# The start of a dense-SiLU backward kernel: x in four tiles on two queues, fewer warm-up matmuls

## The chip, the cores and the metric

The kernel runs on one core of one Trainium2 chip. The metric is device time in microseconds (us), as the median of several executions. The profile of one execution gives a span (first to last instruction); the measured time is about 1.8 us longer, so the two are not mixed here.

## The reference

```python
B, S, D, F = 1, 2048, 640, 1536          # all bfloat16

def _fwd_reference(x, w1, w2):
    h = silu(einsum("bsd,df->bsf", x, w1))
    return einsum("bsf,fd->bsd", h, w2)

def reference(x, w1, w2, grad_out):
    out, vjp = jax.vjp(_fwd_reference, x, w1, w2)
    return (out, *vjp(grad_out))          # out, grad x, grad w1, grad w2
```

## The kernel before

The rows of x are worked off in four chunks of 512. For each chunk the kernel computes h = x·w1, its SiLU and derivative, the output, and the gradient of x; two long stages for the weight gradients follow. Only the start concerns us. The first chunk of x is loaded in its natural layout, transposed on TensorE, and then the first matmuls of h can run. Warm-up matmuls on a tile of zeros keep TensorE busy while the first data travel.

```python
NWARM = 36
warm = cpool.tile([P, P], dt_in, name="warm")
nc.vector.memset(warm[:], 0.0)
warm_a = cpool.tile([P, 1], FP32, name="warm_a")
nc.scalar.activation(warm_a[:], warm[:, 0:1], ACT.Silu)        # loads the Silu table
wp = ps_h.tile([P, SC], FP32, name="wp", tag="hp")
for i in range(NWARM):
    nc.tensor.matmul(wp[:, 0:P], lhsT=warm[:], rhs=warm[:], start=True, stop=True)
# ... cut ...
nc.sync.dma_start(out=x_nat[:, 0:STC, :], in_=x_v[:, 0:STC, :])              # 512 rows, 640 KB
nc.sync.dma_start(out=w1_nat[:, :, 0:FH], in_=w1_v[:, :, 0:FH])              # 320 KB
nc.sync.dma_start(out=w1_nat[:, :, FH:FC], in_=w1_v[:, :, FH:FC])
# ... cut: rest of w1, w2, transposed loads ...
for dt_ in range(DT):                                  # pe_xT: 5 x 4 transposes
    tp = ps_h.tile([P, 4, P], dt_in, name="tp", tag="hp")
    for j in range(4):
        nc.tensor.transpose(tp[:, j, :], x_nat[:, j, dt_ * P:(dt_ + 1) * P], ident[:])
    # DVE (even dt_) or ACT (odd dt_) copies tp to xT[:, dt_, 0:512]
# h_group(ft): five 128x512 matmuls over dt_, then two ACT and two DVE instructions
# ... cut ...
if c == 1:
    for j in range(0, ST, STC):                        # rows of grad_out, four loads
        nc.sync.dma_start(out=go_nat[:, j:j + STC, :], in_=go_v[:, j:j + STC, :])
```

## Time and profile before

| | before |
|---|---|
| median of the first 6 runs | 321.89 us (321.7 to 322.4) |
| span of the profiled run | 320.1 us |
| TensorE (PE) busy | 316.2 us, 99% |
| last row of x's first chunk landed | 5.25 us |
| first matmul of h | 6.42 us |
| end of the last matmul, to the end of the span | 317.43 us, 2.68 us |

These are lines of the page of the profiled run: span, busy times, and the chain of work that ended last, by engine. (PE is TensorE's matmuls, PEld its weight loads, DVE VectorE, ACT ScalarE, POOL GpSimd; SPq is SyncE's sequencer, which issues DMAs and waits; x20 counts instructions; L125 is a line of the kernel. "issue" is time in which the engine waited for nothing that the profile shows. Of the tiles, x_nat is x as loaded, tp what the transposes write, xT the transposed x, wp what the warm-up writes and hp the sums of the matmuls.)

```profile
span 320.1 us, 3590 instructions
PE 316.2 (99%) x1512; PEld 146.7 (46%) x1512; DVE 101.9 (32%) x179; ACT 78.3 (24%) x140; POOL 0.7 (0%) x6
...
PE 98%; DMA 1%; DVE 0%; issue 0%; DVEq 0%
```

TensorE works all the time, and the chain runs through it. The chain in order of time (start in us, length in us, what) shows the only other piece of size, at the very start:

```profile
0.74 4.51 DMA x_nat<-in_x_dram
5.30 1.29 PE tp L125 x20
6.59 12.95 PE hp L151 x60
```

The timeline of PE for the same stretch (start, length, engine, line, output and inputs; in brackets the idle time before and its releaser):

```profile
0.99 4.02 PE L97 MATMUL wp<-warm 128*128 128x128 bf16 x36 [0.99 <-DVE warm L92]
5.30 1.29 PE L125 MATMUL tp<-ident,x_nat 128*128 128x128 bf16 x20 [0.28 <-DMA x_nat<-in_x_dram]
6.42 1.25 PE L151 MATMUL hp<-xT,w_nat 128*128 128x512 bf16 x5
```

Read it so: 36 warm-up matmuls take 4.02 us and start 107 ns apart. The twenty transposes have the same shape and start 56 ns apart: TensorE's clock went from half to full rate in between. Below, "the clock is released" means this change. From 6.42 us the matmuls follow each other without a gap until 317.43 us, those of 128x512 every 216 ns. First h matmul to last matmul is 311.01 us. So the span is a sum of three terms: **start of h + 311.0 + end**.

### The profile page before, as it was taken

How to read it: one execution, taken by the hardware profiler on the slowest of the kernel's cores; microseconds unless marked ns; L12 is line 12 of the kernel's file. 1: busy time of each engine (PE TensorE's matmuls, PEld its weight loads, DVE VectorE, ACT ScalarE, POOL GpSimd, SP SyncE). 2: the span in 40 equal slices, each digit the busy share in tenths (PEclk: the TensorE clock that was granted, in tenths of full speed). 3: DMA queues.
4: the chain of work that ended last, by engine and by line, in shares of the span. 5: the costliest groups of instructions: out<-in, count | busy, mean ns of one | idle time of the engine just before them, and what ended most of it. 6: DMA issues, size and time to landing. Idle time of an engine off the chain costs nothing.

```text
span 320.1 us, 3590 instructions
## 1 busy us (share of the span) xinstructions
PE 316.2 (99%) x1512; PEld 146.7 (46%) x1512; DVE 101.9 (32%) x179; ACT 78.3 (24%) x140; POOL 0.7 (0%) x6
## 2 busy tenths in 40 slices
PE   8999999999999999999999999999999999999996
PEld 7444444444444444444444444444444444444443
DVE  1871551477510087710147751000000100001001
ACT  3960001555201255401154520110100001001100
POOL 0000000000000000000000000000000000000000
DMA  8999999999999855291635079809999999994111
GB/s 232 314 194 190 252 222 274 341 263 309 262 286 296 227 180 151 69 324 63 175 109 146 2 247 269 224 16 301 260 241 242 269 209 342 238 293 166 52 37 47
DMA packets 149200, 66.69 MB, mean 208 GB/s; under 512 B 112576, under 2 KB 149184, under 8 KB 149184
## 3 DMA queue, kind: packets, MB, share of 16 engines
q1 hardware_dynamic: 149184, 66.46, 81.8%
q8 instruction: 12, 0.20, 0.3%
q14 instruction: 4, 0.03, 0.0%
HBM read 9.18 MB, written 28.97 MB: 119 GB/s over the span
## 4 chain that ended last, share of the span: by engine, by line
PE 98%; DMA 1%; DVE 0%; issue 0%; DVEq 0%
PE hp L186 32%; PE hp L151 16%; PE hp L276 16%; PE hp L170 16%; PE hp L324 15%; DMA x_nat<-in_x_dram 1%; PE hp L306 1%; PE tp L125 0%; DVE g_2364 L317 0%; DVEq L317 0%
## 5 line engine op out<-in xcount | busy, mean ns | idle before, releaser
L151 PE MATMUL hp<-xT,w_nat 128*128 128x512 bf16 x240 | 56.9, 379 | 0.0
L170 PE MATMUL hp<-goT,w2T 128*128 128x512 bf16 x240 | 56.9, 379 | 0.0
L186 PE MATMUL hp<-aT,w_nat 128*128 128x512 bf16 x240 | 52.5, 379 | 0.0
L186 PE MATMUL hp<-ghT,w1T 128*128 128x512 bf16 x240 | 52.5, 379 | 0.0
L276 PE MATMUL hp<-a_blk,go_nat 128*128 128x512 bf16 x240 | 52.0, 379 | 0.0
L324 PE MATMUL hp<-gh_blk,x_nat 128*128 128x512 bf16 x224 | 48.5, 379 | 0.0
L194 ACT ACTIVATE oT<-hp 128x512 bf16<-128x512 f32 x24 | 14.3, 597 | 110.0 <-PE hp L186 110.0
L186 PEld LDWEIGHTS <-w_nat 128*128 128x128 bf16 x240 | 23.5, 98 | 28.3
L170 PEld LDWEIGHTS <-w2T 128*128 128x128 bf16 x240 | 23.5, 98 | 28.3
L276 PEld LDWEIGHTS <-go_nat 128*128 128x128 bf16 x240 | 23.5, 98 | 28.3
L186 PEld LDWEIGHTS <-w1T 128*128 128x128 bf16 x240 | 23.4, 98 | 28.4
L158 ACT ACTIVATE aT<-hp 128x512 bf16<-128x512 f32 x48 | 28.7, 598 | 31.1 <-PE hp L151 31.1
L151 PEld LDWEIGHTS <-w_nat 128*128 128x128 bf16 x240 | 23.4, 98 | 28.1
L196 DVE CAST oT<-hp 128x512 bf16<-128x512 f32 x16 | 11.1, 692 | 78.0 <-PE hp L186 78.0
L177 DVE SCALAR_TENSOR_TENSOR ghT<-ghT,hp 128x512 bf16<-128x512 bf16 x48 | 32.5, 683 | 7.3 <-PE hp L170 7.3
L324 PEld LDWEIGHTS <-x_nat 128*128 128x128 bf16 x224 | 21.9, 98 | 26.4
L163 DVE SCALAR_TENSOR_TENSOR ghT<-aT,v 128x512 bf16<-128x512 bf16 x48 | 33.0, 688 | 0.6
L162 DVE TENSOR_SCALAR v<-t 128x512 bf16<-128x512 f32 x48 | 20.5, 427 | 28.5 <-ACT t L160 28.5
L160 ACT ACTIVATE t<-hp 128x512 f32<-128x512 f32 x48 | 28.4, 591 | 0.0
L286 DVE CAST g2T<-hp 128x512 bf16<-128x512 f32 x7 | 4.8, 692 | 46.1 <-PE hp L276 46.1
L284 ACT ACTIVATE g2T<-hp 128x512 bf16<-128x512 f32 x8 | 4.8, 598 | 47.0 <-PE hp L276 47.0
L97 PE MATMUL wp<-warm 128*128 128x128 bf16 x36 | 4.0, 313 | 1.0 <-DVE warm L92 1.0
(32 smaller groups left out, 27.0 us busy)
## 6 DMA issues: line engine op xcount, KB each, us to landing
aT_scr<-aT SPq DMA_DIRECT2D x4, 1536.0 KB, 6.2
ghT_scr<-ghT SPq DMA_DIRECT2D x4, 1536.0 KB, 10.1
out_dram<-o_sb SPq DMA_DIRECT2D x8, 640.0 KB, 3.4
x_nat<-in_x_dram SPq DMA_DIRECT2D x4, 640.0 KB, 4.7
oT_scr<-oT SPq DMA_DIRECT2D x4, 640.0 KB, 4.3
go_nat<-in_grad_out_dram SPq DMA_DIRECT2D x4, 640.0 KB, 7.1
gxT_scr<-oT SPq DMA_DIRECT2D x4, 640.0 KB, 4.7
w_nat<-in_w_dram SPq DMA_DIRECT2D x2, 960.0 KB, 11.3
```

The costliest lines, as they stand in the source:

```text
L151: nc.tensor.matmul(hp[:], lhsT=w1_nat[:, dt_, ft * P:(ft + 1) * P], rhs=xT[:, dt_, :], start=(dt_ == 0), stop=(dt_ == DT - 1),)
L158: nc.scalar.activation(aT[:, ft, :], hp[:], ACT.Silu)
L160: nc.scalar.activation(t[:], hp[:], ACT.Tanh, scale=0.5)
L162: nc.vector.tensor_scalar(out=v[:], in0=t[:], scalar1=-0.5, scalar2=0.5, op0=ALU.mult, op1=ALU.add)
L163: nc.vector.scalar_tensor_tensor(out=ghT[:, ft, :], in0=aT[:, ft, :], scalar=1.0, in1=v[:], op0=ALU.subtract, op1=ALU.mult)
L170: nc.tensor.matmul(gp[:], lhsT=w2T[:, dt_, ft * P:(ft + 1) * P], rhs=goT[:, dt_, :], start=(dt_ == 0), stop=(dt_ == DT - 1),)
L177: nc.vector.scalar_tensor_tensor(out=ghT[:, ft, :], in0=ghT[:, ft, :], scalar=1.0, in1=gp[:], op0=ALU.add, op1=ALU.mult)
L186: nc.tensor.matmul(op_[:], lhsT=w_all[:, ft, dt_ * P:(dt_ + 1) * P], rhs=rhs_all[:, ft, :], start=(ft == 0), stop=(ft == FT - 1),)
L194: nc.scalar.activation(oT[:, dt_, :], op_[:], ACT.Copy)
L196: nc.vector.tensor_copy(out=oT[:, dt_, :], in_=op_[:])
L276: nc.tensor.matmul(gp[:], lhsT=go_nat[:, st, dt_ * P:(dt_ + 1) * P], rhs=a_blk[:, st, :], start=(st == 0), stop=(st == ST - 1),)
L324: nc.tensor.matmul(gp[:], lhsT=x_nat[:, st, dt_ * P:(dt_ + 1) * P], rhs=gh_blk[:, st, :], start=(st == 0), stop=(st == ST - 1),)
```

## The change

The intent is to start h earlier. x comes in four 128-row tiles on two queues (SyncE and ScalarE issue two each), and each tile is transposed as it lands. The first piece of w1 comes as rows 0 and 1 of five, then rows 2 to 4. The warm-up needs no memset, since it reads a constant that exists already, and has 26 matmuls. Four filler matmuls follow the transposes. Here is the diff, cut to its core.

```diff
-    NWARM = 36
+    NWARM = 26
+    NFILL = 4
-        warm = cpool.tile([P, P], dt_in, name="warm")
-        nc.vector.memset(warm[:], 0.0)
+        warm = nc.const_aps.tensor(1.0, (P, P), dt_in)
...
-        nc.sync.dma_start(out=x_nat[:, 0:STC, :], in_=x_v[:, 0:STC, :])
-        nc.sync.dma_start(out=w1_nat[:, :, 0:FH], in_=w1_v[:, :, 0:FH])
+        load_x_tile(nc.sync, 0)
+        load_x_tile(nc.scalar, 1)
+        load_x_tile(nc.sync, 2)
+        load_x_tile(nc.scalar, 3)
+        for lo, hi in ((0, 2), (2, DT)):
+            nc.sync.dma_start(out=w1_nat[:, lo:hi, 0:FH], in_=w1_v[:, lo:hi, 0:FH])
...
+        nc.scalar.activation(warm_a[:], warm[:, 0:1], ACT.Silu)     # moved behind the loads
...
-        xT_next = pe_xT(0, 1)
+        DS = 3
+        def pe_x_tile(xT, st):
+            for lo, hi, copy in ((0, DS, nc.vector.tensor_copy), (DS, DT, nc.scalar.copy)):
+                tp = ps_h.tile([P, hi - lo, P], dt_in, name="tp", tag="hp")
+                for dt_ in range(lo, hi):
+                    nc.tensor.transpose(tp[:, dt_ - lo, :], x_nat[:, st, dt_ * P:(dt_ + 1) * P], ident[:])
+                copy(out=xT[:, lo:hi, st * P:(st + 1) * P], in_=tp[:])
+        for st in range(STC):
+            pe_x_tile(xT_next, st)
+        for i in range(NFILL):
+            nc.tensor.matmul(wp[:, 0:P], lhsT=ident[:], rhs=x_nat[:, STC - 1, 0:P], start=True, stop=True)
```

## The prediction

> **What bounds the kernel now.** TensorE, everywhere but in the first 6.4 us. The page gives PE 316.2 us busy of a 320.1 us span (99%). The chain of waits that ended last is 98% PE; before it stand 4.51 us for the first load of x (0.74 to 5.25 us) and 1.29 us of twenty transposes (from 5.30 us). From there PE runs without a gap to 317.4 us, successive 128x512 matmuls starting 216 ns apart, granted clock 1.00. The waits of PE show only two: 1.0 us for the memset of the warm tile, 0.3 us for x. The change touches the start alone: it can only shift this stream by a fraction of a microsecond, 0.1 to 0.3% of the time.
>
> **What it changes, costed.** In the timeline the 36 warm-up matmuls start at 0.99 us, 107 ns apart, about half rate; the transposes after them 56 ns apart. The 640 KB of x land at 5.25 us; the first w1 piece (320 KB), behind it on the same queue, at about 6.35 us; the first real matmul starts at 6.42 us. So x with its transposes, and w1, limit the start almost together.
>
> 1. Without the memset (DVE, 0.82 to 0.93 us) the warm-up starts 0.2 us earlier; 26 of them (2.8 us) end near 3.6 us. That alone gains nothing.
> 2. x in four 160 KB tiles on two queues: the same bytes at about 350 GB/s, so the last tile should still land at 5.0 to 5.2 us, the first two near 3.8 us. Fifteen transposes happen before the last tile lands. After it remain three transposes before the DVE copy, PE latency and that copy (128x512 took 425 ns, so I estimate 0.35 us for 128x384): first real matmul 0.75 us after the last landing, near 5.8 us.
> 3. w1's rows 0 and 1 of five (128 KB) should land near 5.7 us, the rest near 6.2 us. Two matmuls (0.43 us) run before the rest is needed: an equivalent start near 5.8 us as well.
> 4. Four filler matmuls cost about 0.22 us of PE, hidden behind the DVE copy. Silu's table load (1.28 us) moves behind two DMA issues on ScalarE (a 128-descriptor issue took 0.33 us elsewhere): not critical.
>
> The whole gain is on the critical path, as nothing later waits for DMA: w1's third piece lands at 9.4 us and is needed at about 10.2. I expect the stream 0.5 us earlier.
>
> **Prediction: 321.4 us** (before 321.95), 80% range 320.9 to 322.2. Chances: faster by over 2%: 0.005; within 2%: 0.985; slower by over 2%: 0.01.
>
> **What would show it.** First tile landing before 4 us; transposes from about 3.8 to 5.4 us; first h matmul near 5.8 us, perhaps a gap up to 0.3 us after its second; no PE gaps later; the tail unchanged.
>
> **What would make it wrong.** First, the clock. The Trainium skill, "TensorE: Matmul & The Clock Gate", Part 1, has the array at half clock until about 3.4 us of sustained activity; the trace agrees (107 ns apart up to 4.7 us, 56 ns from 5.3 us). With ten warm-up matmuls fewer and gaps between tiles, full rate may come later; each h matmul at half rate costs about 0.21 us more, so 2 us of delay costs 1 us and turns gain into loss. I give this 15 to 20%. Second, "DMA: Bandwidth & Descriptors", "Issuing engines are not separate DMA queues", has both queues share the same engines: if w1's packets interleave with the last x tiles, these land after 5.25 us and the gain shrinks to 0.2 us.

## The result, and the profile after

| | before | after |
|---|---|---|
| median, 6 runs each | 321.89 us (321.7 to 322.4) | 321.91 us (321.5 to 322.27) |
| ratio after/before | | 0.9999, 95% interval 0.9987 to 1.0012 |
| last row of x's first chunk landed | 5.25 us | 5.50 us |
| first matmul of h | 6.42 us | 6.48 us |
| first h matmul to end of last matmul | 311.01 us | 311.00 us |
| end of last matmul to end of span | 2.68 us | 2.98 us |

A ratio is the mean time of one kernel's runs over that of the other's runs of the same rounds, so it is not quite the ratio of the medians quoted. No gain shows. The interval reaches from 0.42 us faster to 0.39 us slower (0.9987 and 1.0012 of 321.9 us): a small gain could hide in it, but hardly the predicted 0.5 us. The time lies inside the predicted range. The page of after, and its chain at the start:

```profile
span 320.5 us, 3556 instructions
PE 314.0 (98%) x1477; PEld 145.9 (46%) x1506; DVE 101.8 (32%) x179; ACT 78.6 (25%) x142; POOL 0.7 (0%) x6
...
PE 97%; DMA 1%; issue 1%; ACT 0%; SPq 0%; DVE 0%; DVEq 0%
```

```profile
1.19 4.09 DMA x_nat<-in_x_dram
5.27 0.05 issue
5.32 0.47 PE tp L148 x5
5.78 0.02 issue
5.81 0.66 ACT xT L149 x2
6.47 0.01 issue
6.48 0.38 PE hp L161
```

PE has 1477 matmuls here but 1506 weight loads. The records of 29 matmuls are missing, about every fiftieth, and each leaves a gap of twice 216 ns between its neighbours. That is no stall, because the 311.00 us are intact. The timeline of PE:

```profile
0.78 2.93 PE L96 MATMUL wp<-const-bfloat16-1.0 128*128 128x128 bf16 x26 [0.78 <-PEq L362]
3.62 0.74 PE L148 MATMUL tp<-ident,x_nat 128*128 128x128 bf16 x10
5.32 0.73 PE L148 MATMUL tp<-ident,x_nat 128*128 128x128 bf16 x10 [0.96 <-DMA x_nat<-in_x_dram]
5.88 0.39 PE L154 MATMUL wp<-x_nat,ident 128*128 128x128 bf16 x4
6.48 1.24 PE L161 MATMUL hp<-xT,w_nat 128*128 128x512 bf16 x4 [0.21 <-ACT xT L149]
```

The view names ScalarE (ACT) as what released h, and so does the chain. It puts a wait for several semaphores down to the one that came last; point 5 of the account shows that VectorE's copy set the start.

In this one profile the two first tiles are transposed early, as intended. But tile 2 landed at 5.27 us and tile 3 at 5.50 us. A load counts as landed when its sixteen DMA completions are in. For tile 3 fifteen of them were in by 4.95 us, and the last came 0.55 us later; before, this lag was 0.26 us. From the last landing to the first h matmul the new order needs 0.98 us (6.48 − 5.50) where the old one needed 1.17 (6.42 − 5.25). The later landing eats that gain, and the start of h is 0.06 us late.

The end of the span was 0.30 us longer, although the change does not touch it. These are the waits of SyncE's queue at the end, before and then after (who waited for what: us in total, times, longest):

```profile
SPq L363 <- PEq L363: 0.6, 2, 0.4
SPq L363 <- DMA out_dram<-g_2364: 0.5, 1, 0.5
SPq L318 <- DVE g_2364 L317: 0.3, 1, 0.3
SPq L363 <- DMA out_dram<-g_2344: 0.3, 1, 0.3
```

```profile
SPq L373 <- DMA out_dram<-g_2366: 1.1, 1, 1.1
SPq L373 <- PEq L373: 0.6, 2, 0.4
SPq L328 <- DVE g_2366 L327: 0.3, 1, 0.3
```

Before, SyncE waits for the second last store (0.3 us) and then for the last one (0.5 us). After, it waits 1.1 us for the last store at once. The longer wait itself is harmless, for it ends at the same moment (below). What counts is what SyncE still has to do after it.

### The profile page after: what moved, and what is told of

The parts are those of the page before. It is cut to its first block, busy times and chain, and to the rows that moved or that the text cites. A ratio compares the mean times of both kernels' runs of the same rounds, so it can differ in the third digit from the quotient of the medians.

```text
span 320.5 us, 3556 instructions
## 1 busy us (share of the span) xinstructions
PE 314.0 (98%) x1477; PEld 145.9 (46%) x1506; DVE 101.8 (32%) x179; ACT 78.6 (25%) x142; POOL 0.7 (0%) x6
## 4 chain that ended last, share of the span: by engine, by line
PE 97%; DMA 1%; issue 1%; ACT 0%; SPq 0%; DVE 0%; DVEq 0%
PE hp L196 32%; PE hp L180 16%; PE hp L286 16%; PE hp L161 16%; PE hp L334 15%; DMA x_nat<-in_x_dram 1%; PE hp L316 1%; ACT xT L149 0%; PE tp L148 0%; SPq L123 0%; DVE g_2366 L327 0%; DVEq L327 0%
## 5 line engine op out<-in xcount | busy, mean ns | idle before, releaser
L343 ACT ACTIVATE g_2140<-hp 128x512 bf16<-128x512 f32 x1 | 0.6, 597 | 13.6 <-DMA out_dram<-g_2077 13.6
```

## The experiments

Five theories were in play. **A**: a late DMA engine sets the landing of the last tile, however x is split. **B**: the second queue lets w1's packets pass x. **C**: something else than x holds the start. **D**: TensorE's clock is released at a moment that differs from run to run, and the new start is more exposed to it. **E**: the order of the last waits makes the end longer.

### after_again: the changed kernel once more

> The changed kernel once more, for a second profile. In the first one the last x tile landed at 5.50 us (15 of its 16 engine completions by 4.95 us) and the first h matmul started at 6.48 us, against 5.25 and 6.42 before. Both theories expect the same again: last x tile at 5.3 to 5.6 us, one completion 0.4 to 0.7 us behind the other fifteen, first h matmul at 6.4 to 6.6 us, time within 0.1% of before. If landings scatter by more than 0.3 us between the two profiles, single profiles can't settle this.

Measured: 322.09 us median (321.75 to 322.5, 5 runs), ratio 1.0004 (0.9992 to 1.0017). In its profile the last tile landed at 4.78 us, its last completion only 0.09 us behind the other fifteen, and h started at 5.99 us. The expectation missed on both counts: the landing moved by 0.72 us between two profiles of one kernel. So the late landing of the first profile is one draw of a lottery and not a property of the change, and single profiles can't settle the case. Even with h starting 0.43 us earlier than in the first profile of before (6.42 − 5.99), the span was 319.97 us against 320.11, only 0.14 us less: the end took 2.98 us again.

### x_one_queue: all four tiles on one queue

```diff
-        load_x_tile(nc.scalar, 1)
+        load_x_tile(nc.sync, 1)
-        load_x_tile(nc.scalar, 3)
+        load_x_tile(nc.sync, 3)
```

> All four x tiles on the SP queue, ahead of w1. Theory A (one slow DMA engine of sixteen sets the landing of the last tile, however x is split): last tile still at 5.2 to 5.5 us, first h matmul at 6.3 to 6.5 us or later if issuing four tiles in a row (0.4 us each) delays w1; time unchanged within 0.1%. Theory B (the second queue lets packets of w1 pass the last tile): with strict order the last tile lands near 5.0 us, its late completion is gone, first h matmul near 6.0 us, 0.4 us faster.

Measured: 322.82 us median, ratio 1.0026 (1.0012 to 1.004). The last tile landed at 5.51 us and h started at 6.44 us, about as A said, but A's unchanged time did not come. Strict order did not make x earlier in this profile. That alone would not settle B, for the fourth tile was also issued 0.9 us later (2.12 us for 1.20 in the second profile of after). The packets in the traces say more: x comes in packets of 1280 bytes, the first 512 columns of w1 in packets of 512. Before the last x packet started, 352 packets of 512 bytes had started here, 174 and 261 in the two profiles of before, 531 and 140 in the two of after. So w1 passes the tail of x on one queue as well as on two. And in the first profile of after, where x was late, the last twelve x packets of one chain (4.31 to 4.88 us) take 55 ns each and start 51 to 57 ns apart, from the two queues in turn. That is the pace of one engine that still has only x to do. So w1 did not hold that tile up at the end. What moved was w1. Its second piece was issued at 3.08 us for 2.17 us in the second profile of after, and landed at 7.41 us for 6.26. The start of h, at 6.44 us, then stalls:

```profile
6.44 0.38 PE L161 MATMUL hp<-xT,w_nat 128*128 128x512 bf16 x1 [0.21 <-ACT xT L149]
7.45 0.39 PE L161 MATMUL hp<-xT,w_nat 128*128 128x512 bf16 x1 [0.63 <-DMA w_nat<-in_w_dram]
```

The Trainium skill says in "DMA: Bandwidth & Descriptors", section "Issuing engines are not separate DMA queues", that a second issuing engine only saves the issue time, "which is usually small relative to the DMA itself". The trace agrees that issue time is saved (about 0.4 us a tile). At this start one queue instead of two cost 0.7 us on the mean (322.81 us against 322.11 of after_again, run against the same rounds of before). The wait for w1 in this profile is a cause that the trace shows; that it is all of the 0.7 us is not shown.

### x_two_tiles_only: tiles 2 and 3 taken off the path

The transposes of tiles 2 and 3 read tiles 0 and 1, so the result is wrong.

```diff
-  nc.tensor.transpose(tp[:, dt_ - lo, :], x_nat[:, st, dt_ * P:(dt_ + 1) * P], ident[:])
+  nc.tensor.transpose(tp[:, dt_ - lo, :], x_nat[:, st % 2, dt_ * P:(dt_ + 1) * P], ident[:])
-  ... rhs=x_nat[:, STC - 1, 0:P], ...
+  ... rhs=x_nat[:, 1, 0:P], ...
```

> Wrong result on purpose: transposes of tiles 2 and 3 read tiles 0 and 1 (landed at 3.6 and 3.7 us); the loads stay. If the landing of tiles 2 and 3 holds the start (both theories above), the first h matmul moves from 6.48 to about 5.8 us (first w1 piece landed at 5.78), with a wait of about 0.2 us before the third matmul (second w1 piece at 6.43): 0.4 us faster, about 0.12%. If the copies, the clock or w1 hold it (theory C), the h stream starts within 0.15 us of 6.48 us and the time stays.

Measured: 322.01 us median (321.53 to 322.23), ratio 0.9998 (0.9985 to 1.0011). In the profile, which is of the 321.53 us run, h starts at 5.63 us (about 5.8 was expected), followed by about 0.15 us of small stalls for w1. But the median did not fall: the other four runs lie between 321.64 and 322.23. So tiles 2 and 3 can hold the start. What most runs lose by them these five do not tell: their mean, 321.91 us, is 0.20 us below that of after_again, with a scatter of 0.7 us. This scatter pointed to D.

### skip_last_engine: loads that leave out the sixteenth DMA engine

```diff
-            eng.dma_start(out=x_nat[:, st, :], in_=x_v[:, st, :])
+            eng.dma_start(out=x_nat[0:120, st, :], in_=x_v[0:120, st, :])
+        nc.scalar.dma_start(out=x_nat[120:128, 0:STC, :], in_=x_v[120:128, 0:STC, :])
```

The first two pieces of w1 were cut in the same way: 120 rows each, and the last 8 rows of both in one load.

> x tiles and the first two w1 pieces as 120 rows plus 8 rows, so that these loads should run on the first fifteen and first eight DMA engines only, by the rule of the skill's page DMA: Bandwidth & Descriptors. Theory A, if the slow engine is the sixteenth: no completion trails the others by 0.4 us any more, last x tile near 5.0 us, first h matmul near 6.0 us, 0.4 us faster. If the slow engine is another one, or if lateness comes from contention (theory B): a late completion remains and the last tile lands at 5.3 us or later. More issues (0.4 us each) may cost w1 0.3 us.

Measured: 324.06 us median (323.23 to 326.44), ratio 1.006 (1.0043 to 1.0077). As a test of A it failed. The 8-row load of w1 was issued at 3.39 us and landed at 8.11 us, so the start was held by something new. Some loads of 120 rows still had a late completion (0.17 us behind the others for the last x tile, 0.28 us for w1's first piece, at most 0.01 us for the other x tiles), and which engine is late stays unknown. By accident it is the plainest picture of D. In its profile the transposes start 107 ns apart and the h matmuls, from 8.15 us, 427 ns apart; only from 13.6 us on it is 216 ns.

### before_again and before_warm26: the clock in the kernel before

```diff
-    NWARM = 36
+    NWARM = 26
```

> The kernel before against itself: the noise of the comparison, and a second profile of it. Theory D (clock lottery): TensorE gets its full clock at a moment that differs from run to run. So far the full rate came at 3.4 to 4.9 us, and not before 4.7 us in the kernel before, counted from the start; half-rate transposes or matmuls after 5.3 us stretch the start by up to 0.9 us. It expects a ratio within 0.15% of 1, most runs at a floor near 321.7 us and the rest spread up to 322.6, and in the profile successive transposes either 56 or 107 ns apart. Theory A (a late DMA engine alone makes the spread): transposes always 56 ns apart, and the landing of x moves instead, between 5.0 and 5.8 us.

> The kernel before with 26 warm-up matmuls for 36, nothing else; they end near 3.8 us and PE idles 1.5 us until x lands. Theory D: the window in which the clock looks for sustained work (about 3.4 us by the skill's page TensorE: Matmul & The Clock Gate) often holds this gap, so full rate comes late, up to 8 to 10 us, in most runs; transposes 107 ns apart cost 1.0 us, each half-rate h matmul 0.21 us: median 0.7 to 1.8 us slower than before. Theory A (only landings matter): no change, within 0.15%.

Measured: before against itself gives 321.86 us, ratio 1.0004 (0.999 to 1.0018); four of its six runs lie within 321.65 to 321.87, the other two at 322.5 and 322.59. Ten warm-up matmuls fewer, and nothing else, gives 324.03 us median (323.8 to 324.26), ratio 1.0064 (1.0051 to 1.0077): 2.1 us slower on the mean (324.03 − 321.94). x landed at the same time in both profiles, 5.06 and 5.04 us. The timelines of PE, before_again and then before_warm26:

```profile
0.99 3.89 PE L97 MATMUL wp<-warm 128*128 128x128 bf16 x36 [0.99 <-DVE warm L92]
5.11 1.29 PE L125 MATMUL tp<-ident,x_nat 128*128 128x128 bf16 x20 [0.23 <-DMA x_nat<-in_x_dram]
6.24 1.25 PE L151 MATMUL hp<-xT,w_nat 128*128 128x512 bf16 x5
```

```profile
0.99 2.95 PE L97 MATMUL wp<-warm 128*128 128x128 bf16 x26 [0.99 <-DVE warm L92]
5.08 2.32 PE L125 MATMUL tp<-ident,x_nat 128*128 128x128 bf16 x20 [1.14 <-DMA x_nat<-in_x_dram]
7.19 2.34 PE L151 MATMUL hp<-xT,w_nat 128*128 128x512 bf16 x5
```

The same twenty transposes take 1.29 us in one and 2.32 us in the other, and the h matmuls run 427 ns apart until 10.07 us, when the trace's own record has the full clock granted. The start of h comes 0.95 us later (7.19 − 6.24), and the stream from there to the last matmul takes 312.43 us instead of 311.01: together 2.37 us, close to the measured 2.1. Theory D is shown for this kernel. The warm-up is there to cover the way until x lands, and with 26 matmuls a gap of 1.14 us opens. (The mean granted clock listed for this run was 1.00 all the same. The distance between starts shows what that number doesn't.)

The Trainium skill explains it in "TensorE: Matmul & The Clock Gate", Part 1: the array runs at half clock until a window of about 3.4 us was busy, and the window runs freely, so that its borders fall at another moment in each run. The traces agree: from its record to its end the full clock lasted 317.440 us in six profiles, 314.026 us in four and 310.613 us in one, which are 93, 92 and 91 times 3.4133 us.

The same records allow an estimate of how much work releases the clock. In x_two_tiles_only the window that ended with the release ran from 0.02 to 3.43 us, and TensorE had worked in its last 2.66 us. In skip_last_engine, counted back from its release, a window ended at 3.36 us with 2.59 us of warm-up, and the clock stayed at half. In its later windows, and in the other nine records, no window before the release held more than 2.5 us (each matmul counted up to the start of the next, at most 107 ns for a warm-up matmul or transpose and 427 ns for an h matmul). So about 2.6 us of work in one window were enough here, and for a TensorE that works without a pause from 0.77 us on the release falls between about 3.4 and 6.8 us, by the phase of the window alone.

### after_warm36 and after_warm13: the clock in the changed kernel

```diff
-    NWARM = 26
+    NWARM = 36      # or 13
```

> The changed kernel with 36 warm-up matmuls, which end near 4.6 us: the first transposes come 0.6 to 1.0 us later, but PE works without the gap between 3.5 and 4.0 us, and with a shorter one before the third tile. Theory D: the clock is released before the h matmuls in nearly every run; median 321.4 to 321.7, 0.1 to 0.2% faster than the changed kernel and at least not slower than before. Theory A: h start as in the changed kernel or later by the delayed transposes (0 to 0.3 us): 321.9 to 322.2.

> The changed kernel with 13 warm-up matmuls, which end near 2.2 us. x lands and is transposed as in the changed kernel, only the work that wakes the clock is less. Theory D: full rate comes late, during the h matmuls (some 7 to 12 us), in nearly every run: 0.8 to 2.5 us slower than the changed kernel, 322.8 to 324.4 us. Theory A: no change, within 0.15% of the changed kernel.

Measured: with 13, 323.17 us median (322.07 to 323.64), ratio 1.003 (1.0012 to 1.0047), with the clock released at 8.12 us in the profile. D holds for the changed kernel as well. With 36, 322.21 us (321.92 to 322.36, 4 runs), ratio 1.0006 (0.9993 to 1.0019): D expected 321.4 to 321.7, so this expectation missed. Its profile explains one part of the miss: the warm-up delays the first transposes to 4.46 us, h starts at 6.16 us. And it shows the other part once more: the last matmul ended 0.27 us earlier than in the first profile of before (317.16 against 317.43 us), but the span was 320.14 us, not shorter than 320.11. The end took 2.98 us.

### after_tail, before_tail, before_tail_again, after_tail_warm30: the end

Laid side by side, all the profiles of before so far (warm26 included) ended 2.67 to 2.69 us after the last matmul, and all those of after and of its variants with the same number of DMAs 2.96 to 2.99 us. SyncE's instructions in the trace tell why. These are records of the trace, as ns after the last matmul (the last store is issued at 411 to 413 ns in both):

```
before_again                                  after_again
 789  wait semaphores 106 and 105             1901  wait semaphores 104 and 103
 858  wait 107 and 104                        1970  wait 106 and 102
 925  wait 108 and 101                        2036  wait 107 and 100
1293  wait 109 and 100                        2101  wait 108 and 110
1867  wait 110 and 102                        2162  wait 109 and 105
1932  drain, then the closing barriers        2227  drain, then the closing barriers
```

The DMAs take their completion semaphores in turn from a set of eight. At the end SyncE waits for ten semaphores, two in each step, in a fixed order, and each step costs some 65 ns even if nothing is left to wait for. Before, the last store used semaphore 110, which stands in the last step: when it landed, near 1.87 us, everything else had been ticked off while it travelled. With four DMAs more the last store uses semaphore 104, which stands in the first step. It lands near 1.90 us, at about the same time, and four steps (2227 − 1932 = 295 ns in all) come after it. Theory E predicts that four further DMAs anywhere undo it, and that four in the kernel before bring it about. The rows of grad_out are loaded far from any critical moment:

```diff
-                for j in range(0, ST, STC):
-                    nc.sync.dma_start(out=go_nat[:, j:j + STC, :], in_=go_v[:, j:j + STC, :])
+                for j in range(0, ST, STC // 2):
+                    nc.sync.dma_start(out=go_nat[:, j:j + STC // 2, :], in_=go_v[:, j:j + STC // 2, :])
```

> The changed kernel, with the load of grad_out rows in eight pieces for four: nothing but four more DMAs, so that the last DMA of the program uses another of the eight DMA semaphores. Theory E (the order of the last waits): in every profile of the changed kernel the span ends 2.96 to 2.98 us after the last matmul, before 2.67 to 2.69 us, because SyncE waits for ten semaphores in five steps of 65 ns at the end and the semaphore of the last store stands in the first step instead of the last. With four more DMAs it stands in the last again: the end returns to 2.66 to 2.70 us, and the time falls by 0.29 us, to a median of 321.6 to 321.8. Rival (the second DMA queue costs time at the end): the end stays at 2.97 us, time 321.9 to 322.1.

> The converse: the kernel before with the same split of the load of grad_out, four more DMAs on its one queue. Theory E: the semaphore of the last store moves to the first step of the last waits, the span ends 2.94 to 2.99 us after the last matmul instead of 2.68, floor of the times 322.0 instead of 321.7, median 0.2 to 0.35 us slower than before. Rival (second queue): end stays at 2.68 us and the time stays within noise.

> As the first of these, with 30 warm-up matmuls for 26, which end near 4.0 us, when the first tiles have landed: no gap of PE between 3.5 and 3.8 us. If that gap delays the clock (theory D), 0.1 to 0.3 us faster than the first, median 321.4 to 321.7; if the flip comes by its own phase in most runs anyway, the same as the first within 0.15 us. The end as in the first, 2.66 to 2.70 us after the last matmul.

Measured:

| run | end after last matmul | median | ratio to before |
|---|---|---|---|
| after_tail | 2.67 us | 321.44 us (321.27 to 321.89) | 0.9984 (0.9972 to 0.9996) |
| before_tail | 2.94 us | 322.70 us (322.26 to 322.89) | 1.0018 (1.0006 to 1.003) |
| after_tail_warm30 | 2.69 us | 321.52 us (321.08 to 322.14) | 0.9983 (0.9969 to 0.9997) |

The end moved as E says, both ways, and it did so in the kernel before with its single queue, so the second queue is not the cause. An unplanned third case agrees: skip_last_engine has two DMAs more than after, its last store uses semaphore 106, which stands in the third of the five steps there, and its end is 2.82 us, between the two. SyncE's waits at the end of after_tail and then of before_tail have the two forms seen above, exchanged:

```profile
SPq L328 <- ACT g L325: 1.9, 1, 1.9
SPq L373 <- DMA out_dram<-g: 0.8, 2, 0.5
```

```profile
SPq L318 <- ACT g L315: 1.9, 1, 1.9
SPq L363 <- DMA out_dram<-g: 1.1, 1, 1.1
```

The changed kernel with this repair is faster than before by 0.16%, or 0.5 us (0.1 to 0.9); after itself was not (0.9999 and 1.0004). The medians missed the expected ones: 321.44 us lies below 321.6 to 321.8, and that of before_tail is 0.89 us above before (322.70 − 321.81) for 0.2 to 0.35. So after_tail beats before clear of noise, and after by comparison through before: they did not run in the same rounds. after_tail_warm30 did not differ from after_tail (mean 321.57 and 321.52 us), so no gain of four more warm-up matmuls shows.

before_tail was slower than its end explains: 0.61 us on the mean (322.62 − 322.01) for 0.26. Its profile had the clock released late, at 6.32 us, with transposes 107 ns apart up to then, so chance was suspected and the kernel was run again.

> The kernel before with four more DMAs, once more, because its first five runs lay 0.6 us above before on average where the longer end (2.94 us after the last matmul for 2.68) explains 0.27. If the rest was chance (late clock in those runs; in its profile the transposes ran 107 ns apart up to 6.3 us), the lowest time is now near 322.0 us and the mean 0.2 to 0.4 us above before. If the split load of grad_out itself costs time in the kernel before, the lowest stays at 322.2 us or more and the mean 0.5 to 0.7 us above, and a gap between matmuls must show near its issue at 58 to 70 us. The end after the last matmul: 2.94 us again.

Measured: 322.12 us median (321.98 to 322.79, 5 runs), lowest 321.98, mean 0.20 us above before in the same rounds (322.27 − 322.07), end 2.96 us, ratio 1.0006 (0.9993 to 1.002). First h matmul to last matmul was 311.01 us again, so the split of the load costs nothing between. The rest in the first five runs is consistent with chance.

### All profiles, as sums

The time of release is that of the trace's record of the full clock, or, where there is none, of the change from 107 to 56 ns between starts. All in us; skip_last_engine and x_one_queue, held by w1, are left out.

| profile | last x tile landed | clock released | first h | to last matmul | end | span |
|---|---|---|---|---|---|---|
| before | 5.25 | 4.7 to 5.3 | 6.42 | 311.01 | 2.68 | 320.11 |
| before_again | 5.06 | 4.6 | 6.24 | 311.01 | 2.69 | 319.94 |
| before_tail | 4.98 | 6.32 | 6.75 | 311.00 | 2.94 | 320.69 |
| before_tail_again | 5.13 | 4.30 | 6.30 | 311.01 | 2.96 | 320.26 |
| before_warm26 | 5.04 | 10.07 | 7.19 | 312.43 | 2.67 | 322.29 |
| after | 5.50 | 3.67 | 6.48 | 311.00 | 2.98 | 320.46 |
| after_again | 4.78 | 3.78 | 5.99 | 311.00 | 2.98 | 319.97 |
| after_warm36 | 4.81 | 4.30 | 6.16 | 311.00 | 2.98 | 320.14 |
| after_warm13 | 4.73 | 8.12 | 6.58 | 311.75 | 2.99 | 321.31 |
| after_tail | 4.74 | 4.7 | 5.82 | 311.00 | 2.67 | 319.49 |
| after_tail_warm30 | 4.61 | 6.63 | 6.59 | 311.00 | 2.69 | 320.28 |

Two rows show what the clock is worth: after_tail and after_tail_warm30. x landed at 4.74 and 4.61 us, but the clock came at 4.7 and 6.63 us, and h starts 0.77 us apart. Some 0.3 us of this is not the clock: the transposes start at 3.92 us instead of 3.63, behind four more warm-up matmuls and a first tile that landed at 3.84 us instead of 3.58. From the first transpose to the last start it takes 1.54 us in one and 2.03 in the other, and these 0.5 us are the clock's. The timelines of PE:

```profile
3.63 1.76 PE L148 MATMUL tp<-ident,x_nat 128*128 128x128 bf16 x20
5.23 0.39 PE L154 MATMUL wp<-x_nat,ident 128*128 128x128 bf16 x4
5.82 1.89 PE L161 MATMUL hp<-xT,w_nat 128*128 128x512 bf16 x8 [0.21 <-ACT xT L149]
```

```profile
3.92 2.34 PE L148 MATMUL tp<-ident,x_nat 128*128 128x128 bf16 x20
6.06 0.63 PE L154 MATMUL wp<-x_nat,ident 128*128 128x128 bf16 x4
6.59 1.24 PE L161 MATMUL hp<-xT,w_nat 128*128 128x512 bf16 x5
```

The last line of this second timeline is the first h matmul, 0.2 us after the last filler started.

## Why the prediction was right or wrong, point by point

The predicted range held the time and "within 2%" was right, but the stated gain of 0.5 us did not come. The account:

1. **"TensorE, everywhere but in the first 6.4 us": right.** Every profile without half clock or stalls in h has the same 311.0 us from the first h matmul to the last.
2. **"No PE gaps later; the tail unchanged": the second half was wrong, and it is the step that failed.** The tail is longer by about 0.3 us in both profiles of the changed kernel and in all its variants with as many DMAs (2.96 to 2.99 against 2.67 to 2.69 us). The cause is that four DMAs more move the last store to a semaphore that SyncE waits for first instead of last, so that four steps of waiting come after the landing instead of before it. Shown by adding four DMAs elsewhere: 2.67 us in the changed kernel, 2.94 and 2.96 us in the kernel before.
3. **"I expect the stream 0.5 us earlier": the start can gain this; how much it gains on the mean, the runs do not settle.** The shortest spans of the timed runs give it in full: 319.7 us less an end of 2.98 for the changed kernel, 319.9 less 2.68 for before, so the last matmul ended 0.50 us earlier (an estimate, as spans of timed runs are listed to 0.1 us). The first h matmul at 5.82 us in after_tail is the predicted 5.8, but by luck: the tile landed about 0.3 us earlier than predicted and what follows took 0.3 us longer (point 5). The means disagree among themselves. The eleven runs of the changed kernel have a mean of 322.01 us, the seventeen of before in the same rounds 321.95: 0.06 us more with 0.29 us more of end makes a start about 0.23 us earlier. after_tail and after_tail_warm30, whose end is that of before, were 0.49 and 0.44 us faster than before on the mean, so their start gained all of that. These too are estimates, and each of them has a noise of 0.3 us or more: the interval of after_tail alone reaches from 0.1 to 0.9 us. So it is not shown that the start fell short of 0.5 us on the mean.
4. **"First, the clock ... 15 to 20%": the right danger, wrongly imagined.** It was put as a rare large loss. It is a draw in each run: in profiles whose PE had no long gap the full clock came anywhere from 3.4 to 6.6 us. The kernel before needs it at about 5.1 us, when its transposes begin; the changed one has real work from 3.6 us on, so more of its draws should cost something. The pairs above and the two cuts of the warm-up count show that a late clock costs time. That the changed kernel loses more by it than before, on the mean, is argued from these profiles and not shown: the landing of the last tile moved too, from 4.61 to 5.50 us.
5. **"The last tile should still land at 5.0 to 5.2 us": it came earlier in most profiles and later in one** (4.61 to 4.81, and once 5.50 us). The other wrong term is what follows a landing: 0.98 us in the first profile of after for the predicted 0.75, and 1.08 to 1.21 us in after_tail and after_again. The predicted parts were right: from the first transpose of the last tile to the start of DVE's copy 0.37 us (0.40 predicted), and the copy 0.36 us (0.35). Two parts were left out. The last tile's transposes start 0.11 us (after) and 0.20 us (after_tail) after the landing, behind those of the tile before. And h starts 0.15 us after the end of DVE's copy, in every profile with the new order of x but skip_last_engine, where h waits for w1. The views name ScalarE's copy, which ends 0.02 us before h in six profiles. But in after_tail_warm30 and after_warm13 h starts 0.08 us before that copy ends, so it does not wait for it. These are DVE's and ACT's last copies in after_tail_warm30, where h starts at 6.59 us:

```profile
6.09 0.36 DVE L149 COPY xT<-tp 128x384 bf16<-128x384 bf16 x1 [0.18 <-PE tp L148]
6.30 0.37 ACT L149 COPY xT<-tp 128x256 bf16<-128x256 bf16 x1 [0.16 <-PE tp L148]
```

   If tile 2 lands after tile 3, as in after_again, ten transposes are left for the end instead of five.
6. **"If w1's packets interleave with the last x tiles": not what made x late.** They interleave in every profile looked at, in the kernel before too. One queue made w1 later and x no earlier.

So where did the expected gain go? About 0.3 us went to the order of the last waits, which is shown. The remaining 0.2 us lie within the noise of the comparison. Draws of clock and landing move the start by more than that from run to run, but that they took a share of the mean gain is not shown. With the waits undone, the changed kernel is about 0.5 us faster than before. Its median of 321.44 us is the number predicted, partly by luck, as the errors of point 5 cancel.

## What to carry to other kernels

When a change moves the time less than its own stage, sum the span in terms (start, stream, end) and compare each, the untouched ones too: here four more DMAs far from the end made it longer, because their number decides which completion semaphore the last store uses. Then read several profiles before you believe a landing or a clock at the start, and take the clock from the distance between starts of equal matmuls. Let warm-up matmuls reach up to the arrival of the first data: ten of them left out of the old start cost 2.1 us. With the new start, more of them showed no gain (after_warm36, after_tail_warm30).

## What the Trainium skill lacked or had wrong

- I found no page with the cost of the closing waits: at the end SyncE waits for the DMA semaphores in a fixed order, some 65 ns a step, and the position of the last store's semaphore was worth about 0.3 us (2.67 to 2.69 us against 2.94 to 2.99 us).
- "TensorE: Matmul & The Clock Gate", Part 4, says the full clock doesn't engage for transposes in transpose mode. Here transposes (recorded as matmuls against the identity; whether the mode was on, the trace doesn't tell) started 56 ns apart once the clock was released and 107 ns before. In after_tail_warm30 the clock was released at 6.63 us, and of the 3.4 us before that only about the first 0.7 were warm-up matmuls, then came 2.1 us of transposes and 0.4 us of fillers: transposes counted as work.
- The same page, Part 1, has the transition vary by about half a microsecond from run to run. Here it came at 3.4 to 6.6 us in profiles without a long gap of PE, which is 2.7 to 5.9 us after the first warm-up matmul. Its penalty of under 1% of a typical kernel agrees: the worse of the two warm-up cuts cost 0.64%.
- "DMA: Bandwidth & Descriptors", section "Issuing engines are not separate DMA queues", calls the saved issue time usually small. Here it was about 0.4 us for each 128-row tile, and one queue instead of two cost 0.7 us on the mean.
- No page that I found says how far the last of a load's sixteen completions may trail: here 0.01 to 0.7 us behind the fifteenth for the x tiles, differently in each run. Which engine it was, and why, the runs don't show.
